# Twelve chunks of linear attention and two feed-forward layers on one core: all chunks ahead of the first large product

## The chip, the core and the metric

One core of a Trainium2 chip runs the whole program. The metric is the device time of one execution in microseconds (us). The engines are TensorE (PE in the profile, its weight loads PEld), VectorE (DVE), ScalarE (ACT), GpSimd (POOL) and SyncE (SP), whose queue issues nearly all loads.

## What is computed

The reference is a block-wise linear attention with a decay for each head, then two feed-forward layers over 1536 tokens (2 batches of 768) of width 512:

```python
for b in range(nb):                       # blocks of the sequence, per batch and head
    intra = (qb @ kb.T * Dmask) @ vb
    inter = (qb * lam_pow) @ kv_state
    out = intra + inter
    kv_state = lam_block * kv_state + (kb * rev_pow).T @ vb
x = out as (tokens, 512)
x = ELU(x @ w_in) @ w_out                 # w_in 512 x 2048, w_out 2048 x 512
x = softplus(x @ w2_in) @ w2_out
```

## The kernel before

**Tiles.** The tokens are cut in 12 chunks of 128 (6 a batch; `CPB` is 6). Chunks 0 to 3 make the token tile 0 of 512 columns, 4 to 7 tile 1, 8 to 11 tile 2. A hidden layer of 2048 is cut in 16 slices `fc` of 128.

**A chunk.** Chunk `g` has one load of its q and k (`att_load`, 512 KB) and one of its k and v in the other layout (`att_load_kv`, 512 KB). Its steps are `att_s` (scores on PE), `att_mask` (DVE), `att_prep` (q times powers, POOL), `att_prep_k` (k times decay, POOL or ACT), `att_x` (PE: state times q in line 343, then scores times v in line 352), `att_state` (PE line 379, then DVE adds the state and POOL makes the faded copy), and `att_conv` (ACT writes the high part `xh` of the result, DVE the rest `xl`). `att_x` of chunk g needs the state of chunk g-1, which DVE writes. The first chunk of a batch has no line 343, the last no state.

**The products.** Every float32 operand is kept as a high part and a rest, and a product is three matmuls. Step `n` handles one slice for one tile: `m1(n)` is 12 matmuls of 128x512 into a bank, `pointwise1` and `pointwise2` are the ELU (ACT, DVE, POOL), `m2(n)` another 12 matmuls, two steps later (`LAG`). The first four steps are slices 0 to 3 for tile 0.

**Weights.** Slices 0 to 3 of the first layer come in halves (`load_half`, 512 KB; half 0 is `w_in`, half 1 `w_out`). `split_half` turns one into high part and rest in five pieces: two ACT instructions (lines 103, 104), a shift on DVE (line 108), a rounding on DVE (line 114), the high part on ACT (line 117), the rest on DVE (line 120). `half(fc, i, count)` issues the next `count` of these pieces. Below, w(2,0) means half 0 of slice 2.

**Order.** Each engine works through its instructions in the order they are put out. The order is written by hand: `start()` does the set-up and chunks 0 to 3, `early_step(n)` for n from 0 to 7 does chunk n+4 around `m2(n-2)` and `m1(n)`, `att_next` puts the loads out. All loads are in SP's one queue. A load into a buffer that was used before waits there for its readers, and each load also waits for the load eight places ahead of it.

Of the kernel before, what the change touches and what calls it, by code (L numbers as in the profile page):

```python
# [7 lines left out]
F32 = mybir.dt.float32  # L8
# [4 lines left out]
ALU = mybir.AluOpType  # L13
PSUM = bass.MemoryType.PSUM

P = 128
# [16 lines left out]
LAG = 2  # L33
NHALF = 4
RING = 10

STARTS = (
    5, 8, 9, 11, 13, 15, 17, 19, 21, 23, 25, 27, 29, 31, 42, 43, 44, 45, 46, 47, 54, 59, 66, 67, 68, 70, 72, 74)
# [2 lines left out]
def body(ctx, tc, consts, attqk, attkv, w1, w2, out):  # L41
# [28 lines left out]
    def bank(name):  # L70
        return ps_h.tile([P, TT], F32, tag="h", name=name)
# [79 lines left out]
    def load_half(fc, i):  # L151
        key, j = ("a", fc) if fc < 2 and i == 0 else ("b", fc) if fc < 2 else ("c", i) if fc == 2 else ("a", i)
        if key not in spare:
            if key == "a":
                spare[key] = acc.tile([P, 2 * DM], U64, tag="yacc0", name="raw0")
            else:
                spare[key] = stage.tile([P, 2 * DM], U64, tag="raw", name="raw")
        whalf[fc, i] = spare[key][:, DM * j:DM * j + DM]
        nc.sync.dma_start(out=whalf[fc, i], in_=w1[fc][:, DM * i:DM * i + DM])
# [17 lines left out]
    def half(fc, i, count):  # L177
        if (fc, i) not in halves:
            halves[fc, i] = split_half(fc, i)
        for _ in range(count):  # L180
            next(halves[fc, i], None)
# [13 lines left out]
    def setup():  # L195
        A.dma_start(out=const_t, in_=consts)
        A.preload_act_table_set("natural_log_exp_and_others")
        warm(8)
        att_load(0)
        att_load(1)  # L200
        att_load_kv(0)
        att_load(2)
        att_load_kv(1)
        att_load(3)
        att_load_kv(2)
        att_load(4)
        att_load_kv(3)
        load_half(0, 0)

    def decays():  # L210
        for h in range(H):
# [15 lines left out]
    at = {}  # L227


    def early(part, half):  # L230
        if part not in spot:
            spot[part] = xp.tile([P, 2, 2, DM], F32, tag=part, name="early")
        return spot[part][:, half]

    spot = {}

    def att_load(g):
        qk = early("xl2", 0) if g == 3 else ap3.tile([P, 2, DM], F32, tag="qk", name="qk")
        if g == 0:

            V.memset(qk[:, 0, :1], 0.0)
        nc.sync.dma_start(out=qk, in_=attqk[g])
        at[g] = [qk[:, 0], qk[:, 1]]

    def att_load_kv(g):
        kv = early("xh2", g - 2) if g in (2, 3) else ap2.tile([P, 2, DM], F32, tag="kv", name="kv")
        o = slice(0 if g else DM, 2 * DM)
        nc.sync.dma_start(out=kv.rearrange("p two n -> p (two n)")[:, o], in_=attkv[g][:, o])
        at[g] += [kv[:, 0], kv[:, 1]]

    def att_next(g):

        if g == 1:
            att_load(5)
            att_load_kv(4)
            load_half(1, 0)
            load_half(0, 1)
        elif g == 2:
            att_load(6)
            att_load_kv(5)  # L260
            load_half(2, 0)
        elif g > 3:
            if g + 2 < NCHUNK:
                att_load_kv(g + 2)
            if g == 4:
                load_half(1, 1)
            if g + 3 < NCHUNK:
                att_load(g + 3)
            if g < 7:
                load_half(*((3, 0), (2, 1), (3, 1))[g - 4])  # L270

    def att_prep(g):

        if g < NCHUNK and g % CPB:
            q = at[g][0].rearrange("p (a i) -> p a i", a=NPAIR)
            G.tensor_tensor(out=q, in0=q, in1=qpow, op=ALU.mult)

    def att_prep_k(g):
        if g >= NCHUNK or g % CPB == CPB - 1:
            return  # L280
        k = at[g][2].rearrange("p (h d) -> p h d", h=H)
        if g == 0:

            ps = bank("kps")
            for p in range(NPAIR):
                o = slice(P * p, P * p + P)
                T.matmul(ps[:, o], at[g][1][:, o], id_t, start=True, stop=True, is_transpose=True, skip_group_check=True)  # L287
            ps = ps.rearrange("p (h d) -> p h d", h=H)
        else:
            ps = k  # L290
        on_a = H if g in (0, 2) else 0
        if on_a < H:
            r = slice(on_a, H)
            G.tensor_tensor(
                out=k[:, r], in0=k[:, r], in1=kdecay[:, r].unsqueeze(2).to_broadcast([P, H - on_a, D]), op=ALU.mult)
        if on_a:
            for h in range(on_a):
                A.activation(out=k[:, h], in_=ps[:, h], func=AF.Copy, scale=kdecay[:, h:h + 1])

    sc, state, faded = {}, {}, {}  # L300

    def att_s(g):

        if g >= NCHUNK:
            return
        q, k = at[g][:2]
        if g < 7:
            ps = [ps_y.tile([P, 512], F32, tag=f"y{g % 2 * 2 + e}", name=f"sps{e}") for e in range(2)]
        else:
            ps = [bank("sps") for e in range(2)]  # L310
        for p in range(NPAIR):
            o = slice(P * p, P * p + P)
            for e in range(2):
                r = slice(64 * e, 64 * e + 64)
                T.matmul(ps[e][:, o], k[r, o], q[r, o], start=True, stop=True, skip_group_check=True)  # L315
        sc[g] = ps

    def att_mask(g):
        if g >= NCHUNK:
            return  # L320
        ps = sc[g]
        sc[g] = s = ap2.tile([P, 2, NPAIR, P], F32, tag="sc", name="sc")
        part = 2 if g == 0 else NPAIR
        for a in range(0, NPAIR, part):
            r = slice(a, a + part)
            for e in range(2):
                y = ps[e].rearrange("p (a i) -> p a i", a=NPAIR)
                V.tensor_tensor(out=s[:, e, r], in0=y[:, r], in1=dmask[:, e, r], op=ALU.mult)
# [212 lines left out]
        late["acc"] = ctx.enter_context(tc.tile_pool(name="late", bufs=1, reuse_waits="tile"))  # L541
        late["tp"] = ctx.enter_context(tc.tile_pool(name="ltp", bufs=2, reuse_waits="tile"))

    def start():
        setup()
        powers()
        decays()
        att_s(0)
        att_prep_k(0)
        att_mask(0)  # L550
        att_s(1)
        att_prep(1)
        att_mask(1)
        ps = att_x(0)
        att_state(0)
        att_conv(0, ps)
        att_next(0)
        att_prep_k(1)
        for g in range(1, TT // P):
            att_s(g + 1)  # L560
            att_mask(g + 1)
            att_prep(g + 1)
            if g > 1:
                att_prep_k(g + 1)
            if g == 3:
                half(0, 0, 2)
            ps = att_x(g)
            att_state(g)
            if g == 3:
                half(0, 0, 1)  # L570
            att_conv(g, ps)
            if g == 1:
                att_prep_k(2)
            att_next(g)
        half(0, 0, 3)

    def early_step(n):
        g = n + TT // P
        if n >= LAG:
            m2(n - LAG)  # L580
        att_s(g + 1)

        def x_and_state(*between):
            att_prep(g + 1)
            att_prep_k(g + 1)
            ps = att_x(g)
            att_state(g)
            for b in between:
                half(*b)
            att_conv(g, ps)  # L590
            att_next(g)

        if n == 0:
            half(1, 0, 1)
            att_mask(g + 1)
            x_and_state((1, 0, 1))
            half(0, 1, 1)
            half(1, 0, 3)
        elif n == 1:
            pointwise2(n - 1)  # L600
            half(0, 1, 2)
            att_mask(g + 1)
            half(0, 1, 2)
            half(2, 0, 1)
            x_and_state((2, 0, 2))
        elif n == 2:
            half(2, 0, 1)
            half(1, 1, 1)
            pointwise2(n - 1)
            half(2, 0, 1)  # L610
            half(1, 1, 1)
            att_mask(g + 1)
            half(3, 0, 1)
            half(1, 1, 2)
            x_and_state((1, 1, 1), (3, 0, 2))
            half(3, 0, 2)
        else:
            fc = n - 1
            if n < 5:
                half(fc, 1, 1)  # L620
            pointwise2(n - 1)
            if n < 5:
                half(fc, 1, 3)
            att_mask(g + 1)
            if n < 5:
                half(fc, 1, 1)
            w_ops(1, may_start(n))
            x_and_state()
            if n < 5:
                load_w()  # L630
        pointwise1(n, m1(n))

    def may_start(n):
        return wnext[1] < len(wqueue) and n >= STARTS[wnext[1] - NHALF]
# [19 lines left out]


    with tc.manual_schedule():
        start()
        for n in range(8):
            early_step(n)
    close_attention()  # L660
    with tc.manual_schedule(engines={ET.PE, ET.Activation, ET.Pool, ET.SP}):
        for n in range(8, len(order) + LAG):
            step(n)
# [49 lines left out]
```

## Time and profile before

| | |
|---|---|
| median of 3 runs (range) | 571.42 us (571.25 to 571.55) |
| the profiled execution | 571.31 us, its span 569.5 us |
| busy: PE, DVE, ACT, POOL | 564.7, 341.8, 353.9, 170.9 us of the span |
| DMA | 49.60 MB, mean 87 GB/s; 330 and 405 GB/s in the first two fortieths |

The profile is read by the chain that ended last: an engine that is busy all the time on that chain sets the time, and others matter where they make it wait. The start of an instruction and its duration are in us from the start of the span.

### The profile page before, as it was taken

To read this page: it belongs to the slowest core of one execution; us is meant where nothing else is said; L and a number is where in the kernel's file an instruction comes from. 1 tells how busy PE (TensorE), PEld (TensorE's weight loads), DVE (VectorE), ACT (ScalarE), POOL (GpSimd) and SP (SyncE) were. 2 spreads that over 40 slices of the span, in tenths; PEclk is the share of its full clock that TensorE was granted. 3 is DMA by queue.
4 is the path that set the end of the run, shared out by engine and by line. 5 is a ranking of instruction groups with operands and counts; after the bars stand their busy time and mean duration, and the time that the engine had idled before them with its cause. 6 is when DMAs were issued, how large, how long until landed. Compare 5 with 4: busy or idle time off the path is not lost.

```text
span 569.5 us, 7760 instructions
## 1 busy us (share of the span) xinstructions
PE 564.7 (99%) x3031; PEld 467.7 (82%) x3031; DVE 341.8 (60%) x405; ACT 353.9 (62%) x563; POOL 170.9 (30%) x144
## 2 busy tenths in 40 slices
PE   9999999999999999999999999999999999999997
PEld 8888888888888888888888888888888888888886
DVE  6896435545464444012767867665799855656656
ACT  4674547656566564343886976756899755655562
POOL 5546402222122122531532442122221221222210
PEclk9999999999999999999999999999999999999999
DMA  8965502423223222000332201100232000100202
GB/s 330 405 252 205 203 2 75 147 85 138 75 78 144 74 75 74 1 0 1 147 121 102 74 10 64 47 28 2 77 146 74 1 0 1 74 1 0 75 0 75
DMA packets 10693, 49.60 MB, mean 87 GB/s; under 512 B 1184, under 2 KB 1568, under 8 KB 7072
## 3 DMA queue, kind: packets, MB, share of 16 engines
q1 hardware_dynamic: 10368, 48.89, 23.1%
q8 instruction: 24, 0.39, 0.3%
q10 hardware_dynamic: 288, 0.20, 0.2%
q14 instruction: 13, 0.11, 0.1%
HBM read 45.95 MB, written 3.15 MB: 86 GB/s over the span
## 4 chain that ended last, share of the span: by engine, by line
PE 98%; DVE 1%; DMA 0%; issue 0%; DVEq 0%
PE y L489 45%; PE hps L416 16%; PE hps L417 15%; PE hps L418 15%; PE sps L315 2%; PE xps L352 2%; PE xps L343 1%; PE stps L379 1%; DMA const_t<-consts 0%; DVE yacc L536 0%; DVE dmask L212 0%; DVE yacc L491 0%; PE kps L287 0%; DVE yacc L528 0%; DVEq L709 0%
## 5 line engine op out<-in xcount | busy, mean ns | idle before, releaser
L416 PE MATMUL hps<-xh,wh 128*128 128x512 f32 x384 | 150.3, 391 | 0.0
L417 PE MATMUL hps<-xl,wh 128*128 128x512 f32 x384 | 149.5, 389 | 0.0
L418 PE MATMUL hps<-xh,wl 128*128 128x512 f32 x384 | 149.4, 389 | 0.0
L458 POOL TENSOR_TENSOR g<-v,g 128x512 fp32r<-128x512 f32 x48 | 62.4, 1300 | 194.2 <-ACT g L456 189.9
L489 PE MATMUL y<-g,wh 128*128 128x512 f32 x384 | 118.3, 389 | 0.0
L489 PE MATMUL y<-wh,g 128*128 128x512 f32 x382 | 117.7, 389 | 0.0
L458 POOL TENSOR_TENSOR g<-l,g 128x512 fp32r<-128x512 f32 x46 | 60.1, 1307 | 183.5 <-ACT g L456 164.1
L427 ACT ACTIVATE v<-hps 128x512 f32<-128x512 f32 x48 | 28.7, 599 | 101.9 <-PE hps L418 101.8
L451 DVE SCALAR_TENSOR_TENSOR v<-v,hps 128x512 f32<-128x512 f32 x48 | 33.0, 688 | 98.4 <-ACT v L428 98.2
L416 PEld LDWEIGHTS hps<-xh,wh 128*128 128x128 f32 x384 | 72.1, 188 | 15.5 <-issue 0.3
L418 PEld LDWEIGHTS hps<-xh,wl 128*128 128x128 f32 x384 | 72.1, 188 | 15.1
L489 PEld LDWEIGHTS y<-g,wh 128*128 128x128 f32 x384 | 72.1, 188 | 14.9
L489 PEld LDWEIGHTS y<-wh,g 128*128 128x128 f32 x382 | 71.7, 188 | 15.2 <-POOL g L458 0.2
L417 PEld LDWEIGHTS hps<-xl,wh 128*128 128x128 f32 x384 | 72.1, 188 | 14.6
L453 DVE TENSOR_TENSOR l<-l,u 128x512 f32<-128x512 f32 x48 | 75.5, 1574 | 4.4
L445 DVE SCALAR_TENSOR_TENSOR u<-u,e 128x512 f32<-128x512 f32 x48 | 33.6, 700 | 69.3 <-ACT l L439 69.3
L489 PE MATMUL y<-g,wl 128*128 128x512 f32 x192 | 74.7, 389 | 0.0
L489 PE MATMUL y<-wl,g 128*128 128x512 f32 x191 | 74.3, 389 | 0.0
L436 ACT ACTIVATE e<-hps 128x512 f32<-128x512 f32 x48 | 28.6, 597 | 71.2 <-PE hps L418 71.2
L120 DVE TENSOR_TENSOR wl<-c,wh 128x1024 fp32r<-128x1024 f32 (+1 forms) x36 | 48.6, 1349 | 13.8 <-ACT wh L117 13.5
L114 DVE CUSTOM_DVE_ANT_0 c<-r,c 128x2048 uint16<-128x2048 uint16 (+1 forms) x36 | 41.7, 1158 | 4.6 <-ACT c L104 1.7
L489 PEld LDWEIGHTS y<-g,wl 128*128 128x128 f32 x192 | 36.0, 188 | 7.5
(69 smaller groups left out, 604.0 us busy)
## 6 DMA issues: line engine op xcount, KB each, us to landing
raw<-w SPq DMA_DIRECT2D x28, 1024.0 KB, 4.8
qk<-attqk SPq DMA_DIRECT2D x11, 512.0 KB, 5.9
kv<-attkv SPq DMA_DIRECT2D x9, 512.0 KB, 5.5
raw<-w SPq DMA_DIRECT2D x8, 512.0 KB, 8.8
out<-yacc SPq DMA_DIRECT2D x7, 256.0 KB, 2.0
early<-attkv SPq DMA_DIRECT2D x2, 512.0 KB, 8.6
out<-o SPq DMA_DIRECT2D x4, 256.0 KB, 2.3
early<-attqk SPq DMA_DIRECT2D x1, 512.0 KB, 7.4
```

The source lines that it names most:

```text
L114: V.tensor_tensor(out=c, in0=r.bitcast(U32), in1=c, op=ALU.add)
L120: V.tensor_tensor(out=lo, in0=c.bitcast(F32), in1=hi.bitcast(F32), op=ALU.subtract)
L416: T.matmul(ps, wh[fc, 0][:, o], h[:, k, :], start=(k == 0), stop=False)
L417: T.matmul(ps, wh[fc, 0][:, o], l[:, k, :], start=False, stop=False)
L418: T.matmul(ps, wl[fc, 0][:, o], h[:, k, :], start=False, stop=(k == KD - 1))
L427: A.activation(out=v, in_=ps, func=AF.Relu, scale=-1.0)
L436: A.activation(out=e, in_=ps, func=AF.Abs)
L445: V.scalar_tensor_tensor(out=u, in0=u, scalar=-1.0, in1=e, op0=ALU.add, op1=ALU.subtract)
L451: V.scalar_tensor_tensor(out=v, in0=v, scalar=-1.0, in1=ps, op0=ALU.add, op1=ALU.max)
L453: V.tensor_tensor(out=v, in0=v, in1=u[0], op=ALU.subtract)
L458: eng.tensor_tensor(out=g[:, 1], in0=v, in1=g[:, 0].bitcast(F32), op=ALU.subtract)
L489: T.matmul(yps[m], a, b, start=(c == begin and i == 0), stop=(last and i == 2))
```

## The change

All 12 chunks go ahead of `m1(0)`. The loads are put out from a table `LOADS`: 19 at the set-up, 9 behind chunk 3, 4 behind chunk 9. The q, k and v of chunks 3 to 8, and k and v of 2, 10 and 11, get rooms in tiles of weights and of x that are made later. Slices w(0,0) and w(1,0) are converted between chunks 5 to 11 (`PIECES`), the other halves in the first five steps (`HALVES`). `att_prep_k` has all heads on ACT for chunks 0 to 2, then half of the heads on ACT and half on POOL (`att_prep_k2`).

```diff
+LOADS = {
+    0: (("q", 0), ("q", 1), ("k", 0), ("q", 2), ("k", 1), ("q", 3), ("k", 2), ("q", 4), ("k", 3), ("q", 5), ("k", 4),
+        ("q", 6), ("k", 5), ("w", 0, 0), ("q", 7), ("k", 6), ("q", 8), ("k", 7), ("w", 1, 0)),
+    3: (("q", 9), ("k", 8), ("q", 10), ("k", 9), ("q", 11), ("k", 10), ("k", 11), ("w", 2, 0), ("w", 0, 1)),
+    9: (("w", 3, 0), ("w", 1, 1), ("w", 2, 1), ("w", 3, 1)),
+}
...
     def att_load(g):
-        qk = early("xl2", 0) if g == 3 else ap3.tile([P, 2, DM], F32, tag="qk", name="qk")
+        home = {3: ("xl2", 0), 4: ("xl2", 1), 5: ("wh4", 0), 6: ("wh5", 0), 7: ("wh6", 0), 8: ("wh7", 0)}
+        qk = room(*home[g]) if g in home else ap3.tile([P, 2, DM], F32, tag="qk", name="qk")
...
     def att_load_kv(g):
-        kv = early("xh2", g - 2) if g in (2, 3) else ap2.tile([P, 2, DM], F32, tag="kv", name="kv")
+        home = {2: ("xh2", 0), 3: ("xh2", 1), 4: ("wl4", 0), 5: ("wl5", 0), 6: ("wl6", 0), 7: ("wl7", 0),
+                10: ("wh3", 0), 11: ("wl3", 0)}
+        kv = room(*home[g]) if g in home else ap2.tile([P, 2, DM], F32, tag="kv", name="kv")
...
+    PIECES = {5: ((), (0, 0)), 6: ((0, 0), ()), 7: ((0, 0), ()), 8: ((0, 0), (1, 0)), 9: ((1, 0), ()), 10: ((1, 0), ()), 11: ((1, 0), ())}
+
+    def attention():
         setup()
         powers()
         decays()
         att_s(0)
-        att_prep_k(0)
+        att_prep_k(0, att_turn_k())
         att_mask(0)
...
+        for g in range(NCHUNK):
+            before, behind = PIECES.get(g, ((), ()))
             att_s(g + 1)
             att_mask(g + 1)
             att_prep(g + 1)
+            att_prep_k2(g + 1)
+            if before:
+                half(*before, 1 if g in (6, 9) else 2)
             ps = att_x(g)
             att_state(g)
             att_conv(g, ps)
+            att_prep_k(g + 1)
+            if behind:
+                half(*behind, 1)
+            loads(g or None)
+
+    HALVES = {0: ((2, 0),), 1: ((0, 1),), 2: ((3, 0), (1, 1)), 3: ((2, 1),), 4: ((3, 1),)}
 
     def early_step(n):
+        first, *more = HALVES[n]
+        ps = m1(n)
+        half(*first, 1)
+        if n - 1 in mid:
+            pointwise2(n - 1)
+        half(*first, 4)
+        for h in more:
+            half(*h, 1)
+        pointwise1(n, ps)
+        for h in more:
+            half(*h, 4)
         if n >= LAG:
             m2(n - LAG)
+        if n > 2:
+            load_w()
...
     with tc.manual_schedule():
-        start()
+        attention()
+    close_attention()
+    with tc.manual_schedule():
         for n in range(8):
-            early_step(n)
-    close_attention()
+            (early_step if n in HALVES else step)(n)
```

In the built program the order on the engines is not quite that of the text: the conversion of w(2,0), which `early_step(0)` writes behind the attention, stands inside it.

ACT before, where w(2,0) is converted (lines 103 and 104 from `raw_336`, line 117 into `wh2_580`), and what stands around it; `g_494` is `pointwise2(0)`, `xps_509` and `xps_510` are the results of chunk 5, `hps_538` is `m1(1)`:

```order
L456 ACTIVATE g_494<-v_480 128x512
L117 ACTIVATE wh0_394<-r_458 128x512
L103 ACTIVATE r_504<-raw_336 128x512
L104 ACTIVATE c_505<-raw_336 128x512
L366 ACTIVATE xh1_446<-xps_509 128x2x128
L366 ACTIVATE xh1_446<-xps_510 128x2x128
L427 ACTIVATE v_551<-hps_538 128x512
L428 ACTIVATE v_551<-v_551 128x512
L117 ACTIVATE wh2_580<-r_504 128x512
```

ACT now, at chunk 9: `kv_412` is its k and v, `raw0_133` holds w(1,0), `raw_420` holds w(2,0), `xps_699` and `xps_700` are the results of chunk 9, `early_416` is the k and v of chunk 10 (line 111, 112, 125, 357, 284 are the lines 103, 104, 117, 366, 298 of before):

```order
L284 ACTIVATE kv_412<-kv_412,kdecay_93 128x64 x4
L111 ACTIVATE r_679<-raw0_133 128x512
L112 ACTIVATE c_680<-raw0_133 128x512
L111 ACTIVATE r_841<-raw_420 128x512
L112 ACTIVATE c_842<-raw_420 128x512
L125 ACTIVATE wh2_847<-r_841 128x512
L357 ACTIVATE xh2_669<-xps_699 128x2x128
L357 ACTIVATE xh2_669<-xps_700 128x2x128
L284 ACTIVATE early_416<-early_416,kdecay_93 128x64 x4
L125 ACTIVATE wh1_757<-r_679 128x512
```

The two first instructions and the high part of w(2,0) have moved from step 1 to between the k of chunk 9 and the results of chunk 9.

DVE before, at the shift and the rounding of w(2,0) (lines 108 and 114 on `r_504`, `c_505`), with the mask of chunk 6 ahead and the rest of the results of chunk 5 behind:

```order
L328 TENSOR_TENSOR sc_499<-sps0_483,dmask_92 128x512
L328 TENSOR_TENSOR sc_499<-sps1_484,dmask_92 128x512
L120 TENSOR_TENSOR wl0_395<-c_459,wh0_394 128x512
L108 TENSOR_SCALAR r_504<-r_504 128x512
L114 ISA c_505<-r_504,c_505 128x1024
L367 TENSOR_TENSOR xl1_447<-xps_509,xh1_446 128x2x128
L367 TENSOR_TENSOR xl1_447<-xps_510,xh1_446 128x2x128
L451 SCALAR_TENSOR_TENSOR v_551<-v_551,hps_538 128x512
L120 TENSOR_TENSOR wl2_581<-c_505,wh2_580 128x512
```

DVE now: `r_679` and `c_680` are w(1,0), `r_841` and `c_842` w(2,0); `state_726` is the state of chunk 9, `state_787` that of chunk 10, `sc_752` the masked scores of chunk 11 (lines 116, 122, 128, 376, 358, 319 are 108, 114, 120, 385, 367, 328 of before):

```order
L116 TENSOR_SCALAR r_679<-r_679 128x512
L116 TENSOR_SCALAR r_841<-r_841 128x512
L122 ISA c_842<-r_841,c_842 128x1024
L376 TENSOR_TENSOR state_726<-stps_717,faded_667 128x256
L358 TENSOR_TENSOR xl2_670<-xps_699,xh2_669 128x2x128
L358 TENSOR_TENSOR xl2_670<-xps_700,xh2_669 128x2x128
L128 TENSOR_TENSOR wl2_848<-c_842,wh2_847 128x512
L319 TENSOR_TENSOR sc_752<-sps0_742,dmask_92 128x512
L319 TENSOR_TENSOR sc_752<-sps1_743,dmask_92 128x512
L122 ISA c_680<-r_679,c_680 128x1024
L376 TENSOR_TENSOR state_787<-stps_778,faded_728 128x256
```

The shift and the rounding of w(2,0) stand ahead of the state of chunk 9, and the state of chunk 10 stands behind the rest of w(2,0), the mask of chunk 11 and the rounding of w(1,0).

SP now, the nine loads of `loads(3)`: `qk_406`, `qk_410`, `qk_414` are q and k of chunks 9 to 11, `kv_408`, `kv_412`, `early_416`, `early_418` k and v of chunks 8 to 11, and the last two w(2,0) and w(0,1):

```order
L250 DMA qk_406<-attqk 128x1024
L258 DMA kv_408<-attkv 128x1024
L250 DMA qk_410<-attqk 128x1024
L258 DMA kv_412<-attkv 128x1024
L250 DMA qk_414<-attqk 128x1024
L258 DMA early_416<-attkv 128x1024
L258 DMA early_418<-attkv 128x1024
L167 DMA raw_420<-w1 128x512
L167 DMA raw_422<-w1 128x512
```

The load of w(2,0) is the 27th of the queue; before, it was the 17th, behind k and v of chunk 5.

## Rows read from the trace of the kernel before

**Rows 1.** The page: span, PE's busy time, the chain that ended last

```profile
span 569.5 us, 7760 instructions
PE 564.7 (99%) x3031; PEld 467.7 (82%) x3031; DVE 341.8 (60%) x405; ACT 353.9 (62%) x563; POOL 170.9 (30%) x144
PE 98%; DVE 1%; DMA 0%; issue 0%; DVEq 0%
```

**Rows 2.** Timeline, PE, 9 to 19 us: start, us, engine, line, operation

```profile
9.05 1.16 PE L315 MATMUL sps<-qk 64*128 64x128 f32 x16
10.14 0.67 PE L343 MATMUL xps<-qk,state 64*64 64x128 f32 x16
10.74 1.09 PE L352 MATMUL xps<-sc,kv 128*64 128x128 f32 x16
11.66 0.64 PE L379 MATMUL stps<-kv 128*64 128x64 f32 x16
12.23 1.16 PE L315 MATMUL sps<-early 64*128 64x128 f32 x16
...
15.41 1.16 PE L315 MATMUL sps<-qk 64*128 64x128 f32 x16
```

**Rows 3.** Timeline, PE, chunks among the steps; then two pieces of the chain

```profile
50.27 1.16 PE L315 MATMUL sps<-qk 64*128 64x128 f32 x16
...
59.11 1.16 PE L315 MATMUL sps<-qk 64*128 64x128 f32 x16
```

```profile
89.59 2.72 PE y L489 x12
...
95.03 2.72 PE y L489 x12
```

**Rows 4.** Timeline, ACT, DVE and POOL, 9 to 20 us

```profile
10.24 1.29 DVE L328 TENSOR_TENSOR sc<-sps,dmask 128x512 f32<-128x512 f32 x2
11.28 1.28 POOL L276 TENSOR_TENSOR qk<-qk,qpow 128x512 f32<-128x512 f32 x1
11.88 0.66 ACT L366 ACTIVATE xh<-xps 128x256 fp32r<-128x256 f32 x2 [2.52 <-PE xps L352]
12.42 0.42 DVE L385 TENSOR_TENSOR state<-stps,faded 128x256 f32<-128x256 f32 x1 [0.88 <-PE stps L379]
12.43 2.01 ACT L298 ACTIVATE early<-early,kdecay 128x64 f32<-128x64 f32 x8
12.76 0.75 DVE L367 TENSOR_TENSOR xl<-xps,xh 128x256 fp32r<-128x256 f32 x2
17.02 0.63 POOL L389 TENSOR_TENSOR faded<-state,qpow 128x256 f32<-128x256 f32 x1
```

**Rows 5.** Timeline, SP: two loads issued; then their time to landing (the last number)

```profile
6.94 0.46 SPq L248 DMA_DIRECT2D early<-attkv  x1
...
28.40 0.42 SPq L159 DMA_DIRECT2D raw<-w  x1
```

```profile
early<-attkv SPq DMA_DIRECT2D x1, 512.0 KB, 9.0
```

```profile
raw<-w SPq DMA_DIRECT2D x1, 512.0 KB, 6.9
```

**Rows 6.** Windows: the stretch, busy time of five engines, PEclk, DMA share, GB/s

```profile
10.00:20.00 10.00, 10.00 (x208) 8.80 (x210) 8.11 (x16) 5.68 (x17) 7.36 (x9) 1.00 1.03 414
20.00:30.00 10.00, 10.00 (x118) 8.07 (x108) 9.38 (x19) 7.49 (x15) 5.75 (x5) 1.00 1.01 391
```

**Rows 7.** Timeline, ACT and DVE, 48 to 51 us: a half converted

```profile
48.89 0.65 ACT L103 ACTIVATE r<-raw 128x512 f32<-128x512 f32 x1
49.62 0.42 DVE L108 TENSOR_SCALAR r<-r 128x512 uint32<-128x512 uint32 x1
50.17 0.69 DVE L114 CUSTOM_DVE_ANT_0 c<-r,c 128x1024 uint16<-128x1024 uint16 x1
50.54 0.62 ACT L117 ACTIVATE wh<-r 128x512 fp32r<-128x512 f32 x1
```

**Rows 8.** The last matmul; then windows of the end (PEclk third from last)

```profile
565.46 0.28 PE L526 MATMUL yh<-wl,g 128*128 128x256 f32 x1
```

```profile
567.00:568.00 1.00, 0.00 (x0) 0.00 (x0) 0.00 (x0) 0.00 (x0) 0.00 (x0) 0.96 1.02 351
568.00:569.00 1.00, 0.00 (x0) 0.00 (x0) 0.00 (x0) 0.00 (x0) 0.00 (x0) 0.50 0.14 44
```

**Rows 9.** Timeline, PE: the warm-up ahead of the first scores

```profile
0.77 3.75 PE L193 MATMUL warm<-const-float32-0.0 128*128 128x128 f32 x16 [0.77 <-PEq L704]
```

More of the change, by code (lines that the diff above doesn't have):

```diff
@@ L198, in setup @@
         warm(8)
[L199 to L208, printed above, removed]
+        loads(0)
     def decays():
@@ L227, in body, with loads, room @@
     at = {}
[L230 to L233, printed above, removed]
     spot = {}
+    def loads(g):
+        for load in LOADS.get(g, ()):
+            {"q": att_load, "k": att_load_kv, "w": load_half}[load[0]](*load[1:])
+    def room(part, half):
+        if part[0] == "x":
+            if part not in spot:
+                spot[part] = xp.tile([P, 2, 2, DM], F32, tag=part, name="early")
+            return spot[part][:, half]
+        return wp.tile([P, 2, DM], F32, tag=part, name="early")
     def att_load(g):
-        qk = early("xl2", 0) if g == 3 else ap3.tile([P, 2, DM], F32, tag="qk", name="qk")
+        home = {3: ("xl2", 0), 4: ("xl2", 1), 5: ("wh4", 0), 6: ("wh5", 0), 7: ("wh6", 0), 8: ("wh7", 0)}
+        qk = room(*home[g]) if g in home else ap3.tile([P, 2, DM], F32, tag="qk", name="qk")
         if g == 0:
@@ L249, in att_load_kv @@
         at[g] += [kv[:, 0], kv[:, 1]]
[L251 to L270, printed above, removed]
     def att_prep(g):
@@ L276, in att_prep, with att_turn_k, k_heads, att_prep_k @@
             G.tensor_tensor(out=q, in0=q, in1=qpow, op=ALU.mult)
-    def att_prep_k(g):
+    def att_turn_k():
+        ps = bank("kps")
+        for p in range(NPAIR):
+            o = slice(P * p, P * p + P)
+            T.matmul(ps[:, o], at[0][1][:, o], id_t, start=True, stop=True, is_transpose=True, skip_group_check=True)
+        return ps
+    def k_heads(g):
+        return H if g < 3 else H // 2
+    def att_prep_k(g, source=None):
         if g >= NCHUNK or g % CPB == CPB - 1:
@@ L281, in att_prep_k, with att_prep_k2 @@
         k = at[g][2].rearrange("p (h d) -> p h d", h=H)
[L282 to L298, printed above, removed]
+        y = k if source is None else source.rearrange("p (h d) -> p h d", h=H)
+        for h in range(k_heads(g)):
+            A.activation(out=k[:, h], in_=y[:, h], func=AF.Copy, scale=kdecay[:, h:h + 1])
+    def att_prep_k2(g):
+        if g >= NCHUNK or g % CPB == CPB - 1 or k_heads(g) == H:
+            return
+        k = at[g][2].rearrange("p (h d) -> p h d", h=H)
+        r = slice(k_heads(g), H)
+        G.tensor_tensor(
+            out=k[:, r], in0=k[:, r], in1=kdecay[:, r].unsqueeze(2).to_broadcast([P, H - k_heads(g), D]), op=ALU.mult)
     sc, state, faded = {}, {}, {}
@@ L306, in att_s @@
         q, k = at[g][:2]
[L307 to L310, printed above, removed]
+        ps = [ps_y.tile([P, 512], F32, tag=f"y{g % 2 * 2 + e}", name=f"sps{e}") for e in range(2)]
         for p in range(NPAIR):
@@ L542, in close_attention @@
         late["tp"] = ctx.enter_context(tc.tile_pool(name="ltp", bufs=2, reuse_waits="tile"))
-    def start():
+    PIECES = {5: ((), (0, 0)), 6: ((0, 0), ()), 7: ((0, 0), ()), 8: ((0, 0), (1, 0)), 9: ((1, 0), ()), 10: ((1, 0), ()), 11: ((1, 0), ())}
+    def attention():
         setup()
@@ L548, in start @@
         att_s(0)
-        att_prep_k(0)
+        att_prep_k(0, att_turn_k())
         att_mask(0)
[L551 to L559, printed above, removed]
+        for g in range(NCHUNK):
+            before, behind = PIECES.get(g, ((), ()))
             att_s(g + 1)
@@ L562, in start @@
             att_prep(g + 1)
[L563 to L566, printed above, removed]
+            att_prep_k2(g + 1)
+            if before:
+                half(*before, 1 if g in (6, 9) else 2)
             ps = att_x(g)
             att_state(g)
-            if g == 3:
-                half(0, 0, 1)
             att_conv(g, ps)
[L572 to L575, printed above, removed]
-    def early_step(n):
-        g = n + TT // P
+            att_prep_k(g + 1)
@@ L580, in early_step @@
             m2(n - LAG)
[L581 to L630, printed above, removed]
@@ L631, in early_step @@
-        pointwise1(n, m1(n))
+        if n > 2:
+            load_w()
     def may_start(n):
```

## The prediction

> **What bounds the kernel now.** I read the page first. PE is busy for 564.7 us of a span of 569.5, and the chain that ended last is PE for 98% [rows 1]. So only two things move the time: PE's own time between its matmuls, and a wait that reaches PE. An idle DVE, ACT or POOL costs nothing, but an instruction that blocks one of them costs all that PE must wait for it.
>
> Then the timeline of the chunks that stand alone. The scores of three successive chunks start at 9.05, 12.23 and 15.41, so a full pass (scores of chunk g+1, then the state part, the score part and the state product of chunk g) takes 3.18 us: 1.09, 0.60, 0.92 and 0.57, from start to start [rows 2]. PE is the bound there too: each starts where the one before leaves off. Among the steps the scores of two chunks lie 8.84 us apart, while a step alone takes 95.03 - 89.59 = 5.44 (24 matmuls) [rows 3]. A chunk among the steps thus costs 3.40, a chunk among chunks 3.18.
>
> **Part 1, chunks joined.** Full passes from 9.05 on: passes 1 to 4 end at 21.77; pass 5 has no state product (2.61), pass 6 no state part (2.58), which gives 26.96; passes 7 to 10 end at 39.68; pass 11 is only its two parts (1.52), so the last chunk ends at 41.20. Then `m1(0)`, 0.1 late for the change of shape (my estimate from half of 3.40 - 3.18), starts at 41.3. From there to `m2(8)` are 11 + 8 groups of 2.72, 51.7 us: 93.0. Before, `m2(8)` starts at 95.03 [rows 3]. Saved if nothing waits: **2.0 us**.
>
> **Part 2, the other engines in a pass.** DVE needs 1.29 + 0.42 + 0.75 = 2.46, ACT 0.66 for the results and 4 x 0.25 for half the heads (8 took 2.01), POOL 1.28 + 0.63 and half the heads, which I put at half of q's product, 0.64: 2.55 [rows 4]. All are under 3.18. The pieces of w(0,0) and w(1,0) add at most 0.7 to DVE and 1.3 to ACT in a pass. Cost: nothing, as long as no piece waits for its load. What hides them is 0.7 us of slack on DVE in each pass; a piece that waits takes the state, which stands behind it, with it.
>
> **Part 3, the loads.** The 9th load (k and v of chunk 3) is issued at 6.94 and lands 9.0 later, at 15.94; the 24th at 28.40 + 6.9 = 35.30 [rows 5]. That is 1.29 us a load of 512 KB, and DMA is at its limit meanwhile: shares of 1.03 and 1.01 at 414 and 391 GB/s [rows 6]. The first nine loads keep their order, and the buffers let later ones go out sooner, so I keep the pace: load number i lands at 15.94 + 1.29 (i - 9). q of chunk 9 is the 20th: 30.1, wanted at 26.96 + 3.18 = 30.14. q of chunk 11 is the 24th: 35.3, wanted at 36.50. So the chunks get their loads with little to spare, at no cost. **w(2,0) is the 27th: 39.2.**
>
> **Part 4, the first new wait.** In the built order ACT converts w(2,0) ahead of the results of chunk 9, and DVE shifts and rounds it ahead of the state of chunk 9. PE wants that state when the scores of chunk 11 are done, at 36.50 + 1.09 = 37.59. From the first ACT instruction of a half to its rounding on DVE are 50.17 - 48.89 = 1.28 us, and the rounding takes 0.69 [rows 7]; so the state starts at 39.16 + 1.97 = 41.13 and ends 0.42 later [rows 4]. PE goes on at 41.6: a stall of **4.0 us**. Queued behind the waiting ACT are the results of chunk 9 and k of chunk 10; both are still in time for their readers.
>
> **Part 5, the second new wait.** From the state of chunk 9 to that of chunk 10 DVE now has: state 0.42, the rests of chunk 9 0.75, the rest of w(2,0) 0.69 (taken as the rounding), the mask of chunk 11 1.29, the rounding of w(1,0) 0.69, the state 0.42: 4.26. Starts come some 0.08 before the end of the one ahead (12.42 + 0.42 against 12.76 [rows 4]), five times: 3.86. So it ends at 45.0, and the state part of chunk 11 goes then. PE itself would be there at 41.6 + 0.60 + 0.92 + 0.57 = 43.7: **1.3 us**. `m1(0)` follows at 45.0 + 1.52 + 0.1 = 46.6, against 41.3 without waits: 5.3 us.
>
> **Part 6, the first steps.** Without a chunk among them the steps are short. From the end of `m1(0)` to `m2(1)` PE has four groups, 10.9 us; ACT has three halves, w(0,1), w(3,0) and w(1,1), of about 1.9 (0.65 + 0.67 + 0.62, from 48.89 to 51.2 with another one between) [rows 7], and eight ELU instructions of 0.62: 10.7. That just fits, with handovers between DVE and ACT in it. Between 0 and 0.6; I take 0.3, since the load of none of these is late by the pace above (w(1,1), the 30th, 43.0).
>
> Without the clock: -2.0 + 5.3 + 0.3 = **+3.6 us**.
>
> **Part 7, the clock.** The trace of before has no stall like the first one. What it has is the end: PE starts its last matmul at 565.46, and the granted clock goes to 0.96 in 567 to 568 and 0.50, the 1.2 GHz level, from 568 on [rows 8]. PE's idle stretch there is shorter than 4.0 us, so I expect the clock to fall in the stall. From below: it doesn't, 0. From above: all of the work from there to `m1(0)`, 2.09 + 1.52, takes twice as long, 3.6 more, of which the second wait swallows 1.3: 2.3. In between: at the start PE warms up for 3.75 us [rows 9] and is quick afterwards; if the low level lasts like that, the 2.09 us become 4.2, chunk 10's state product ends at 45.8, its state 0.5 later, and chunk 11 goes on at 46.3 and not 45.0. I take that, **+1.3**, as the row of the start is the nearest. The Trainium skill (TensorE: Matmul & The Clock Gate, on how the oscillation bites in real kernels) tells of a kernel in which every burst behind a wait for a transfer starts at the low clock. By it the burst of chunk 11 would be slow as well, at the upper bound: 577.2; no row of before shows it.
>
> **Sum.** +4.9 on the profiled execution's 571.31 us (span 569.5) gives **576.2 us**. The median of the runs, 571.42, stands 0.1 above the profiled one, which changes nothing. A measurement of this kernel tells about 0.2%, 1.1 us, from no change.
>
> **Rivals.**
> - *The clock stays up.* Both waits come, but PE keeps 2.4 GHz: 571.3 + 3.6 = **574.9**. For it: the clock is 1.00 in both stages of [rows 6], and the end is one case only. Against: that very case [rows 8]. 27%.
> - *Not slower: w(2,0) is there when ACT comes to it.* ACT has the results of chunk 8, half of the k of chunk 9 and w(1,0) before it: 30.14 + 1.09 + 1.52, then 0.66 + 1.0 + 1.3, so it is free at about 35.8. If the load has landed by then, the state of chunk 9 ends at 35.8 + 1.97 + 0.42 = 38.2 (0.6 us of stall), the second wait keeps its 1.3, and -2.0 + 1.9 + 0.3 is +0.2: **571.5**, no change. It decides at a landing by 36: 18 loads in 20 us, 1.11 us each or 470 GB/s. Against it: the 414 and 391 GB/s of full queues [rows 6]. 8%.
> - *Loads finish out of order.* The Trainium skill (DMA: Bandwidth & Descriptors, on queues, rings and completion order) says that completion is not FIFO for an issuing engine. If w(2,0) overtook the seven loads ahead of it, the time would again be **571.5**. The loads of rows 5 are 15 places apart and land 19.4 us apart, as an orderly queue would have it. 3%.
> - *Still later loads.* The chunks' loads have no slack, and if each took 0.08 more (the 391 against the 414 GB/s is 6%), w(2,0) would land 1.4 later, and the first wait would be as much longer: 576.2 + 1.4 = **577.6**. 8%.
>
> **How the numbers follow.** The forecast has 54% (its own range 575.2 to 577.6). It, the quick clock and the late loads are slower by over 0.2%: 89%. The other two, 11%, end about at no change; I give 7% to the same and 4% to faster, as the saving of 2.0 us is sure. The range is 573.6 to 578.6: below, the quick clock with a landing 1.3 us sooner; above, the late loads with the clock's upper bound. It leaves out the two cases at 571.5 and some tails.
>
> **What would show it.** In the profile after: scores of chunk 11 at about 36.5, then no matmul until about 41.6, ended by DVE's state; ACT idle until w(2,0) lands near 39.2; a second gap of PE, or none if the clock is low; PEclk under 1.00 near 40 to 46; `m1(0)` at 46.5 to 48 and from there groups of 2.72 as before. Wrong would be: a landing before 37, PE without a gap at 37.6, or gaps of PE among the first steps longer than 0.6.

## The result, and the profile after

| | before | after |
|---|---|---|
| median (range, executions) | 571.60 us (571.25 to 572.92, 8) | 576.25 us (575.00 to 580.05, 8) |
| ratio, 95% interval | | 1.0083 (1.0059 to 1.0107) |
| the profiled execution, its span | 571.31, 569.5 us | 575.07, 573.3 us |

The changed kernel is slower by 4.7 us, against +4.9 on the profiled 571.31 in the prediction. But the profiled execution of the changed kernel is one of its fastest, and the gap of 1.2 us between it and the median is the part of the story that the prediction had only half right: the clock.

The page, span, engines and the chain that ended last, against [rows 1]:

```profile
span 573.3 us, 7779 instructions
PE 563.6 (98%) x3031; PEld 468.6 (82%) x3031; DVE 341.7 (60%) x407; ACT 361.3 (63%) x597; POOL 165.3 (29%) x143
PE 91%; DMA 6%; DVE 1%; issue 0%; ACT 0%; SPq 0%; DVEq 0%; ACTq 0%
```

PE has 1.1 us less to do, and the span is 3.8 longer: PE waits. The chain, 98% PE before, is now 6% DMA, and its pieces say which transfer (start, us, what):

```profile
28.77 10.21 DMA raw<-w
...
54.98 2.72 PE y L480 x12
60.52 2.72 PE y L480 x12
...
98.60 2.72 PE y L480 x12
```

`raw<-w`, landed at 38.98, is w(2,0). The last row is `m2(8)`: 98.60 against 95.03 [rows 3], 3.6 us later. PE's waits in total (releaser; us in total, times, longest) have one new large line:

```profile
PE xps L334 <- DVE state L376: 4.6, 2, 3.4
```

PE around the two waits (timeline: start, us, what, and in brackets the idle time before and its releaser; line 334 is the state part, 306 the scores, 343 the score part, 370 the state product, 407 to 409 `m1`):

```profile
36.99 1.16 PE L306 MATMUL sps<-qk 64*128 64x128 f32 x16
41.51 0.67 PE L334 MATMUL xps<-qk,state 64*64 64x128 f32 x16 [3.36 <-DVE state L376]
42.11 1.09 PE L343 MATMUL xps<-sc,early 128*64 128x128 f32 x16
43.03 0.64 PE L370 MATMUL stps<-early 128*64 128x64 f32 x16
44.91 0.67 PE L334 MATMUL xps<-qk,state 64*64 64x128 f32 x16 [1.24 <-DVE state L376]
45.50 1.09 PE L343 MATMUL xps<-sc,early 128*64 128x128 f32 x16
46.53 0.50 PE L407 MATMUL hps<-xh,wh 128*128 128x512 f32 x1
```

ACT and DVE in the same stretch (ACT 111 and 112, DVE 116 and the first 122 convert w(2,0); the second 122 rounds w(1,0); 376 is the state, 128 the rest of a half, 319 the mask):

```profile
39.08 0.66 ACT L111 ACTIVATE r<-raw 128x512 f32<-128x512 f32 x1 [2.78 <-DMA raw<-w]
```

```profile
39.78 0.43 DVE L116 TENSOR_SCALAR r<-r 128x512 uint32<-128x512 uint32 x1 [2.77 <-ACT r L111]
40.34 0.69 DVE L122 CUSTOM_DVE_ANT_0 c<-r,c 128x1024 uint16<-128x1024 uint16 x1
40.95 0.42 DVE L376 TENSOR_TENSOR state<-stps,faded 128x256 f32<-128x256 f32 x1
41.28 0.74 DVE L358 TENSOR_TENSOR xl<-xps,xh 128x256 fp32r<-128x256 f32 x2
41.95 0.68 DVE L128 TENSOR_TENSOR wl<-c,wh 128x512 fp32r<-128x512 f32 x1
42.54 1.28 DVE L319 TENSOR_TENSOR sc<-sps,dmask 128x512 f32<-128x512 f32 x2
43.74 0.68 DVE L122 CUSTOM_DVE_ANT_0 c<-r,c 128x1024 uint16<-128x1024 uint16 x1
44.34 0.42 DVE L376 TENSOR_TENSOR state<-stps,faded 128x256 f32<-128x256 f32 x1
```

Read it upwards from PE: PE stands from 38.15 to 41.51 for the state of chunk 9; the state stands on DVE behind two pieces of w(2,0); these stand behind ACT, which stands for the load. Nothing of w(2,0) is wanted by PE before the third step: a transfer that PE did not need yet holds PE up, because of where its conversion stands. In this execution the clock stays up meanwhile (windows: stretch, busy time of PE, PEld, DVE, ACT, POOL, then PEclk, DMA share, GB/s):

```profile
40.00:42.00 2.00, 0.49 (x16) 0.46 (x16) 1.86 (x6) 2.00 (x7) 0.56 (x1) 1.00 1.02 401
```

### The profile page after: what moved, and what is told of

Same layout as the page of the kernel before. It is cut to its first block, busy times and chain, and to the rows that moved or that the text cites. A ratio compares the mean times of both kernels' runs of the same rounds, so it can differ in the third digit from the quotient of the medians.

```text
span 573.3 us, 7779 instructions
## 1 busy us (share of the span) xinstructions
PE 563.6 (98%) x3031; PEld 468.6 (82%) x3031; DVE 341.7 (60%) x407; ACT 361.3 (63%) x597; POOL 165.3 (29%) x143
## 4 chain that ended last, share of the span: by engine, by line
PE 91%; DMA 6%; DVE 1%; issue 0%; ACT 0%; SPq 0%; DVEq 0%; ACTq 0%
PE y L480 45%; PE hps L407 15%; PE hps L408 15%; PE hps L409 15%; DMA raw<-w 4%; DMA early<-attkv 2%; DMA kv<-attkv 1%; DVE yacc L527 0%; DVE sc L319 0%; PE xps L343 0%; SPq L250 0%; DVE state L376 0%; DVE c L122 0%; DVE yacc L482 0%; PE xps L334 0%
## 5 line engine op out<-in xcount | busy, mean ns | idle before, releaser
L128 DVE TENSOR_TENSOR wl<-c,wh 128x1024 fp32r<-128x1024 f32 (+1 forms) x36 | 50.0, 1389 | 14.4 <-ACT wh L125 14.0
```

What stands on the lines that cost most here:

```text
L128: V.tensor_tensor(out=lo, in0=c.bitcast(F32), in1=hi.bitcast(F32), op=ALU.subtract)
```

## Experiments

The theory: the first wait is the landing of w(2,0), reached through the order of ACT and DVE; the second is DVE's queue; what goes beyond 575 us is PE's clock, which falls while PE stands idle. The rivals: the order does no harm, and the loads, or the steps without chunks among them, cost the time; or the spread has another cause. Each kernel ran beside the kernel before on the same chip; the first four shared one chip (before: 571.92 us, 23 executions), the next three another (571.95, 14), the last a third (571.84, 15).

**The changed kernel once more**, with another profile.

> The changed kernel once more, so that the others have it beside them on one chip. Theory (two waits behind w(2,0), and a clock that falls in the first of them in some executions): 575.0 us in executions whose granted clock is 0.999, and more where it is lower, about 1 us for each 0.002 to 0.003 of mean clock; the median between 575 and 577. Rival (the spread is nothing to do with the clock): the time varies by some us with the clock at 0.999 throughout.

Measured: 577.06 us (575.70 to 579.13, 6 executions), ratio 1.0090 (1.0073 to 1.0107). The median lies just above the expected range, since none of the six shows a clock of 0.999; the time follows the clock as expected. Its profile (span 576.5) caught what the first one did not. PE, then the windows:

```profile
41.50 1.13 PE L334 MATMUL xps<-qk,state 64*64 64x128 f32 x16 [3.09 <-DVE state L376]
42.56 1.97 PE L343 MATMUL xps<-sc,early 128*64 128x128 f32 x16
44.32 1.07 PE L370 MATMUL stps<-early 128*64 128x64 f32 x16
46.08 1.13 PE L334 MATMUL xps<-qk,state 64*64 64x128 f32 x16 [0.69 <-DVE state L376]
```

```profile
39.00:40.00 1.00, 0.00 (x0) 0.00 (x0) 0.24 (x1) 0.93 (x2) 0.00 (x0) 1.00 1.10 414
40.00:41.00 1.00, 0.00 (x0) 0.00 (x0) 0.86 (x3) 1.00 (x3) 0.00 (x0) 0.74 0.94 360
41.00:45.00 4.00, 3.50 (x46) 3.20 (x48) 3.41 (x8) 2.28 (x9) 2.32 (x2) 0.50 0.68 277
45.00:50.00 5.00, 4.31 (x42) 3.36 (x39) 2.11 (x6) 0.90 (x3) 0.00 (x0) 0.50 0.01 3
50.00:51.00 1.00, 1.00 (x4) 0.80 (x3) 0.33 (x1) 0.00 (x0) 0.00 (x0) 0.64 0.00 0
51.00:52.00 1.00, 1.00 (x6) 0.80 (x6) 0.00 (x0) 0.00 (x0) 0.00 (x0) 1.00 0.00 0
```

The same wait, ended at the same time (41.50 and 41.51), but the clock is at 0.50, the 1.2 GHz level, from 41 to 50. Line 334 takes 1.13 us and not 0.67, line 343 1.97 and not 1.09; the second wait shrinks from 1.24 to 0.69, and the first microseconds of `m1(0)` are slow too. `m2(0)`, at 54.98 above, starts here at 58.26 (the chain): the fall costs 3.3 us. (The execution's time is 4.1 us longer, 579.13 against 575.07, its span 3.2: the rest lies outside the span.) Over all 14 executions of the changed kernel, on two chips, the time goes with the mean granted clock:

| mean granted clock | executions | us |
|---|---|---|
| 0.999 | 3 | 575.0 to 575.2 |
| 0.997 | 5 | 575.7 to 576.9 |
| 0.994 | 4 | 577.2 to 577.4 |
| 0.991 and 0.990 | 2 | 579.1 and 580.1 |

Of the executions with a fall one trace of this kernel is kept, that at 0.991. The kernel before shows 0.998 to 1.000 in all of the 52 executions beside the experiments.

**The conversion of w(2,0) back in its place.** Attention and the first steps stand in one hand-ordered block, so each engine keeps the order of the text:

```diff
     with tc.manual_schedule():
         attention()
-    close_attention()
-    with tc.manual_schedule():
         for n in range(8):
             (early_step if n in HALVES else step)(n)
+    close_attention()
```

> The chunks stay joined and the loads stay as they are, but attention and the first steps stand in one hand-ordered block, so that the conversion of w(2,0) stands where the text has it, behind chunk 11, and no longer ahead of the state of chunk 9. Theory (the order, with the landing of w(2,0), costs the time): no gap of PE at chunk 10, the second gap gone too, m1(0) at 41.6 to 41.8, and 570.3 to 571.2 us, that is 575.0 less the 4.8 of the two gaps, plus up to 0.8 for a fourth half among the first steps. Rival (joined chunks are slow in themselves, by loads without slack or by the other engines): at least 574.

Measured: 571.47 us (571.00 to 572.44, 12 executions), ratio 0.9991 (0.9983 to 1.0000). PE:

```profile
37.09 1.16 PE L306 MATMUL sps<-qk 64*128 64x128 f32 x16
38.18 0.67 PE L334 MATMUL xps<-qk,state 64*64 64x128 f32 x16
38.77 1.09 PE L343 MATMUL xps<-sc,early 128*64 128x128 f32 x16
39.70 0.63 PE L370 MATMUL stps<-early 128*64 128x64 f32 x16
41.02 0.67 PE L334 MATMUL xps<-qk,state 64*64 64x128 f32 x16 [0.69 <-DVE state L376]
```

No first wait, and 5.6 us less than the changed kernel beside it (3.6 less than its executions at 0.999, on another chip), with all loads, rooms and pieces of the change in place. Up to the first steps the order differs from that of the changed kernel in nothing but the six instructions that convert w(2,0), three on ACT and three on DVE; behind them, two copies of `m2` results go from DVE to ACT. That settles the cause: not the chunks' loads, not the steps without chunks, but six instructions at a place where they wait for their load. Which part of the edit put them back, the joined block or the later `close_attention()`, was not tried apart. The expectation was missed by 0.3 us: the second gap shrank and did not go. The 0.69 that is left is the state of chunk 10 itself: in the last pass PE has no scores to do while DVE makes it.

**PE kept busy in the wait.** 14 matmuls on zeros behind the scores of chunk 11, nothing else changed:

```diff
             att_s(g + 1)
+            if g == 10:
+                warm(14)
             att_mask(g + 1)
```

On PE they stand ahead of the state part of chunk 10.

> The changed kernel with 14 more matmuls of zeros, as those of the start, between the scores of chunk 11 and the state part of chunk 10, where PE waits for 3.4 us. They write a bank that is free there and take about 3 us. Theory (an idle PE lets the clock fall, by chance of when): granted clock 0.999 in all executions, the time 575.0 to 575.4 in all of them, the spread of some us gone. Rival (the spread comes from loads or from the chip): the spread stays as in the kernel without them, and the clock column with it.

Measured: 575.24 us (575.12 to 575.42, 5 executions), ratio 1.0059 (1.0047 to 1.0071), clock 1.000 in each. PE (each of the 14 shows as two):

```profile
38.44 3.39 PE L201 MATMUL warm<-const-float32-0.0 128*128 128x128 f32 x28
41.76 0.67 PE L334 MATMUL xps<-qk,state 64*64 64x128 f32 x16
```

Useless work does not shorten the wait, but the spread, 3.4 us among the six executions of the changed kernel on this chip, is 0.3. So what lies above some 575.4 us in the changed kernel goes with a clock that falls while PE stands.

**The load of w(2,0) at other places of the queue**, the order of ACT, DVE and PE left as it is (in the last of the three, pieces of w(2,0) move a little). Two places sooner:

```diff
-    3: (("q", 9), ("k", 8), ("q", 10), ("k", 9), ("q", 11), ("k", 10), ("k", 11), ("w", 2, 0), ("w", 0, 1)),
+    3: (("q", 9), ("k", 8), ("q", 10), ("k", 9), ("q", 11), ("w", 2, 0), ("k", 10), ("k", 11), ("w", 0, 1)),
```

> In the queue of loads w(2,0) stands two places sooner, ahead of k and v of chunks 10 and 11, with no other change; the order on the engines is the same. Theory (its landing sets the first wait): it lands 2 x 1.29 = 2.6 us sooner, near 36.5, the gap of PE at chunk 10 shrinks from 3.4 to 0.8 us, the second gap stays at 1.2 us, and the time is 575.0 - 2.6 = 572.4 us with the clock at 0.999 in all executions, since no gap is long. Rival (the order on the engines alone costs the time, whatever the landing): 574.5 to 575 us.

One place sooner (`("w", 2, 0)` behind `("k", 10)`):

> w(2,0) one place sooner, ahead of k and v of chunk 11; order on the engines as in the changed kernel. Theory (the first wait is the landing of w(2,0), one place of the queue is 1.3 us): ACT starts w(2,0) near 37.8, the state part of chunk 10 goes on near 40.3, the first wait is 2.1 us and the second keeps 1.2: 575.0 - 1.3 = 573.7 at the full clock. Rival (finishing order is not queue order, or k and v of chunk 11 become the wait instead): 575 or more. On the clock: if it is the length of the idle stretch that lets it fall, a wait of 2.1 us should show it in few executions or none, a median within 0.4 of the fastest.

One place later (`("w", 2, 0)` behind `("w", 0, 1)`):

> w(2,0) one place later, behind w(0,1). Theory: ACT starts it near 40.4, PE's first wait is 4.7 us: the fastest executions at 575.0 + 1.3 = 576.3; the clock falls in more of them than in the changed kernel, a median of 578 or more. Rival (wait set by something else than the landing): 575.0 to 576.2, as the changed kernel.

Measured:

| w(2,0) | ACT starts it | first, second wait of PE | median (range, executions) | ratio, interval |
|---|---|---|---|---|
| two sooner | 36.27 | 1.24, 1.24 | 573.13 (572.75 to 573.48, 11) | 1.0020 (1.0012 to 1.0029) |
| one sooner | 38.00 | 2.08, 1.24 | 574.03 (573.85 to 574.83, 5) | 1.0044 (1.0032 to 1.0056) |
| as changed | 39.08 | 3.36, 1.24 | 576.25 (575.00 to 580.05, 8) | 1.0083 (1.0059 to 1.0107) |
| one later (clock at 0.50 behind the wait) | 40.82 | 4.80, 0.69 | 578.73 (577.25 to 581.49, 6) | 1.0122 (1.0099 to 1.0145) |

ACT's row of each, two sooner, one sooner and one later:

```profile
36.27 0.69 ACT L111 ACTIVATE r<-raw 128x512 f32<-128x512 f32 x1 [0.39 <-DMA raw<-w]
```

```profile
38.00 0.66 ACT L111 ACTIVATE r<-raw 128x512 f32<-128x512 f32 x1 [1.68 <-DMA raw<-w]
```

```profile
40.82 0.66 ACT L111 ACTIVATE r<-raw 128x512 f32<-128x512 f32 x1 [4.23 <-DMA raw<-w]
```

Three places move ACT by 4.55 us, 1.5 a place (single steps 1.1 to 1.7, from one profile each), and each first wait follows. The load is thus the wait, and it keeps its place in the queue. (In the profiles of "one sooner" and "one later" PE also waits 0.31 and 0.49 us at chunk 9, for its k from POOL: the slack of Parts 2 and 3 was thin, but the first wait ends with w(2,0) all the same.) At "one later" no execution has a clock of 0.999: three show 0.997, three 0.990 or 0.991, and the fastest took 577.25 us where 576.3 was expected for the full clock. At "one sooner" three of five show 0.999 or 1.000 and two 0.997, and those two are the slowest (574.71, 574.83); where in them it fell is not on record. At "two sooner" all eleven show 0.998 to 1.000. So the spread goes with the wait as well. "Two sooner" saves less of the first wait than its load came sooner: PE comes 0.23 us sooner, and k of chunk 10 lands late instead, POOL works on it beside DVE, and the rounding takes 1.10 us, not 0.69. So 573.13, not the 572.4 that was expected:

```profile
37.52 0.61 POOL L291 TENSOR_TENSOR early<-early,kdecay 128x256 f32<-128x256 f32 x1 [1.02 <-DMA early<-attkv]
```

```profile
37.58 1.10 DVE L122 CUSTOM_DVE_ANT_0 c<-r,c 128x1024 uint16<-128x1024 uint16 x1 [0.15 <-ACT c L112]
```

**`m1(0)` ahead of chunk 11.** One block as above, and the last uncovered state covered:

```diff
+            if g == NCHUNK - 1:
+                first_ps.append(m1(0))
             ps = att_x(g)
...
-        ps = m1(n)
+        ps = first_ps.pop() if first_ps else m1(n)
```

> Attention and first steps in one hand-ordered block, and m1(0) ahead of the two parts of chunk 11. Theory (in the one-block kernel the 0.69 us wait for the state of chunk 10 is there because pass 11 has no scores to cover it): m1(0) covers it, no wait at chunk 11, m2(0) near 50.3, and 571.5 - 0.6 = 570.9, against 571.9 of the kernel before: ratio 0.998. Rival (the time is made up later, among the first steps, where ACT has three halves to convert): 571.5, ratio 0.999.

Measured: 572.90 us (572.64 to 574.36, 8 executions), ratio 1.0022 (1.0012 to 1.0032). A miss: chunk 11 no longer waits, but two new waits come, and the reason stands on ACT:

```profile
44.11 0.67 PE L334 MATMUL xps<-qk,state 64*64 64x128 f32 x16
...
52.42 0.51 PE L480 MATMUL y<-g,wh 128*128 128x512 f32 x1 [0.36 <-POOL g L449]
...
56.44 0.50 PE L409 MATMUL hps<-xh,wl 128*128 128x512 f32 x1 [0.46 <-DVE wl L128]
```

```profile
45.85 0.66 ACT L357 ACTIVATE xh<-xps 128x256 fp32r<-128x256 f32 x2 [4.37 <-PE xps L343]
46.39 0.66 ACT L111 ACTIVATE r<-raw 128x512 f32<-128x512 f32 x1
```

ACT idles for 4.4 us with w(2,0) landed, since the conversion stands behind the results of chunk 11, which now come 3 us later (42.76 with one block alone). In the first steps ACT does not make that good. The two waits are 0.8 us; `m2(8)` is 2.4 us later than in the profile of one block (97.11 against 94.74). Of that 0.5 is the start of the program (last section), and the rest is not taken apart here.

**The same, with the conversion of w(2,0) and the ELU of slice 0 ahead of chunk 11 too.**

```diff
+            if g == NCHUNK - 1:
+                first_ps.append(m1(0))
+                half(2, 0, 5)
+                pointwise1(0, first_ps[0])
             ps = att_x(g)
...
     def early_step(n):
+        if n == 0:
+            return
```

> As the kernel with m1(0) ahead of chunk 11, but the conversion of w(2,0) and the ELU of slice 0 also ahead of the results of chunk 11. Theory (m1(0) covers the state of chunk 10; what e7_m1_first lost was the conversion of w(2,0), which stood behind the results of chunk 11 on ACT and so came 3.1 us later): no wait at chunk 11 and none over 0.3 us among the first steps, 571.5 - 0.7 = 570.8, ratio to before 0.998. Rival (the first steps are short of ACT's time wherever the conversion stands): waits of 0.4 to 0.9 at m2(0) and m1(3) as in e7_m1_first, 571.5 or more.

Measured: 570.67 us (570.40 to 571.95, 11 executions), ratio 0.9983 (0.9974 to 0.9992): faster than the kernel before by 1.2 us beside it, and than the changed kernel, whose fastest execution took 575.00. PE's only wait in the list is that of the start:

```profile
PE warm L201 <- PEq L661: 0.8, 1, 0.8
```

```profile
94.15 2.72 PE y L480 x12
```

`m2(8)` is at 94.15, 0.88 sooner than before [rows 3].

## Why the prediction was right, and where it was not

**What bounds, Part 2.** Right. The scores of chunks 2 and 11 start 27.54 us apart (9.45 and 36.99) against 27.45 by the passes of [rows 2]. The 0.1 stands in the pass without a state product (2.71 us for 2.61); the passes with pieces of the first two halves take 3.18, as without.

**Part 1, 2.0 saved.** Right in kind, too large in size. The kernel with no wait at all gains 1.2 us by the medians, and 0.88 at `m2(8)` of the two profiles. Of the 1.1 that is missing there, 0.56 is the start of the program: its first scores take 1.84 us against 1.16 before, which puts the scores of chunk 2 at 9.61 against 9.05 [rows 2].

```profile
4.79 1.16 PE L315 MATMUL sps<-qk 64*128 64x128 f32 x16 [0.27 <-DVE dmask L212]
```

```profile
4.67 1.84 PE L306 MATMUL sps<-qk 64*128 64x128 f32 x16
```

Another 0.17 is a reading: the sum ends at a start in the timeline, but 95.03 is the chain's; the timeline has `m2(8)` of before at 94.86. The rest lies in small parts where the shapes change. Part 1 also left out that pass 11 has nothing to cover the state of chunk 10: 0.69 us with one block. In the changed kernel all this hid in the two waits, whose ends do not depend on when PE came.

**Part 3, the loads.** Right: w(2,0) at 39.2 by the pace of [rows 5], ACT on it at 39.08. The chunks' loads cost PE nothing new: 0.33 us ahead of the first scores, where it had waited 0.27 before for another releaser.

**Parts 4 and 5, the two waits.** Right in cause, place and end: PE goes on at 41.51 (41.6) and 44.91 (45.0). The first stall is 3.4 us and not 4.0, since PE came 0.5 later (scores of chunk 11 at 36.99, not 36.50, 0.4 of it from the start of the program); the end of a wait for a transfer does not care. The DVE queue from state to state takes 44.34 - 40.95 + 0.42 = 3.81 us (3.86).

**Part 6, first steps.** Right in size, not in cause: from 46.53 to `m2(8)` are 51.9 us by the timeline (52.1 to the chain's 98.60), 0.2 above the 51.7, where 0.3 was taken. But PE has no wait in that stretch; the handovers between ACT and DVE that were to cost it do not reach PE. 0.13 is the first group, which takes 2.85 us and not 2.72.

So "without the clock", 574.9 us, is what the three executions at 0.999 took (575.0 to 575.2, the profiled one among them).

**Part 7, the clock.** This is the step that failed, though its value came out well. It took one price, +1.3, and an upper bound of 2.3, "all of the work from there to `m1(0)`". The runs show a spread: none of it in 3 of 14 executions, 0.6 to 2.3 us in nine, 4 to 5 in two (against 575.1; by their spans 3.2 and 5.0). The bound broke because the low level did not end with the attention: in the profile with the fall it lasts some 10 us, into `m1(0)`, and costs 3.3. The 3.75 us of the warm-up in [rows 9], taken for the length of the low level, are only the duration of those matmuls (the last section has what the records of the clock say of the start). The end of the kernel [rows 8] showed rightly that the clock can fall in so short a stall, not that it must. The forecast and the rival "the clock stays up" were therefore not two kernels but two executions of one. That the median came near 576.2 is in part luck: it lies in the middle of that spread (576.25 in eight executions, 577.06 in the next six), and no single price makes it.

The Trainium skill (TensorE: Matmul & The Clock Gate, on the oscillation) tells of a kernel in which every burst behind a wait for a transfer starts cold. The profile with the fall agrees, chunk 11 included (1.13 us at 46.08); the first profile, with the same wait at a clock of 1.00, does not. By that rule the sum gave 577.2; the medians were 576.25 and 577.06.

**The rivals.** "w(2,0) is there when ACT comes" did not happen; two places sooner shows what it would have been worth, 573.1 beside 571.9: ACT started at 36.27, and the first wait was 1.24 us where the rival had 0.6. Against "loads finish out of order" speak the three moves: the landing went with the place in the queue each time. That completion is not FIFO for an issuing engine, as the Trainium skill has it (DMA: Bandwidth & Descriptors, on queues, rings and completion order), no run here shows. Later loads: 39.08, no.

## What to carry to other kernels

Read the built order, not the text: where two hand-ordered blocks met here, instructions that wait for a late load were put in front of some that were wanted now, and the whole chain behind them then waited for that load. To find such a wait, compute the landing from the queue's pace and compare it with the time at which the engine reaches the instruction; the landing came out right to 0.2 us here, ACT's arrival (36.3, as its 2.78 us of idle time say, for 35.8) to 0.5. And a stall of PE of some microseconds is not one price but a spread: quote the time with the clock up, and what an execution with a fall adds, apart.

## What the runs showed of the hardware that was not expected

- The clock does not fall in each such stall. After waits of 3.36 and 3.09 us that end at the same time, it is 1.00 in one profile and 0.50 for some 10 us in the other, from 40.5 to 50.7, where PE had stood for 2.1 us when it fell. In the profile of "one later" it is 0.50 as long, from 41.3 to 51.6. With PE kept busy it stayed at 1.00 in all five executions. After waits of 2.08 us it was low in two executions of five, by the mean clock alone. What decides whether it falls was not found.
- The first microseconds run slow, and the views hide it. The trace's first record of the granted clock, at the 2.4 GHz level, begins at 4.71 us in the profile of before, and between 3.8 and 6.8 in all ten; ahead of it there is no record, and PEclk prints 1.00. But matmuls take up to twice the time there: in the profile of "one later" those of the warm-up start 0.21 us apart up to 3.7 and 0.12 apart behind it, and the record begins at 3.76. The first scores took 1.16 us where the record begins by 4.8, 1.50 and 1.94 in the two profiles of the changed kernel (record from 5.59 and 6.34), 1.84 in the last kernel (6.12), and 2.08 in the one with `m1(0)` moved alone (6.76). The start thus shifts a profile by up to 0.9 us; compare times within a profile from the scores of chunk 2 on.
- The rounding on DVE took 1.10 us beside POOL's product for k, 0.69 alone. In other profiles it took 0.90 and 1.17 at w(0,0), beside POOL's product for q, but 0.69 beside the last product of the ELU (line 449). That the two slow each other was seen in these places, not tried by itself.
